# Routing and ranking for pairs of token groups, running counts on TensorE, one reciprocal buffer

## The chip, the cores and the metric

The kernel runs on 1 core of a Trainium2 chip. The metric is the device time of one execution in microseconds (us); the number quoted is the median of three runs.

## What is computed

Three stages follow each other; the first feeds the second, the second the third.

```python
# 1 attention with a decaying state: 4 batches, 8 heads, 768 tokens, 48 wide
for t in range(S):
    state = alpha[:, :, t, :, None] * state + einsum('bhd,bhe->bhde', k[:, :, t], v[:, :, t])
    y[:, :, t] = einsum('bhd,bhde->bhe', q[:, :, t], state)
# 2 gated dense block on 3072 tokens of 384
x = (((x @ w1) * (x @ w2)) @ w3) @ w_out
# 3 eight experts of 384 -> 1024 -> 384, two per token
noisy = x @ w_gate + log1p(exp(x @ w_noise)) * noise
top2 = the two largest of noisy; weights = softmax over these two
out[token] += weight * (relu(x @ ew1[e]) @ ew2[e])
```

## The kernel before

**Groups.** The 3072 tokens go through in 8 groups of 384 (three tiles of 128), two groups to a batch. For each group attention runs in three chunks: `prep_decay` and `prep_qk` (decay products as scans on VectorE), `scores`, `ktok`, `mix`, `state`, `xturn`. Then come the dense units: sixteen `wide` units of nine matmuls (L532 to L534), and six `narrow` units of twelve (L556 to L558), which give the tile `x2` with 384 outputs and 16 logits per token.

**Routing.** The last `narrow` unit of a group calls `finish`. It scales the logits (L577), splits the outputs into two halves of 16 bits (`split`, ScalarE L181 and VectorE L185) through a tile `xr` of two buffers, writes them to the table of tokens `x2s` from SP's queue (L583), and calls `route`. `route` is a chain of VectorE instructions on 128x24 tiles: logarithm, noise, the two largest, one-hot masks `oh`, weights. At its end (L645 to L648) it keeps a running count `R` per partition and expert: for each of three tiles a copy of `R` into `M[:, 1, t]` and an addition of the tile's mask to `R`.

**Ranking.** `rank(g)` is a unit of its own: two TensorE matmuls (L657, L658) turn the masks and the running counts into each token's place in its expert's list; ten VectorE instructions make addresses; six indirect DMAs on POOL's queue (L686) scatter the tokens' numbers and weights. `rank(g - 1)` stands in group g's units behind the seventh pair of `wide` units, in the last group behind the fifth; group 7 is ranked among the experts. After the scatters of group 0 `clear` zeroes the output: a memset, five DMAs of 960 KB (L518) and one of 192 KB, all on POOL's queue.

**Order.** TensorE's order is written out by hand (`manual_schedule`): attention units and dense units have costs, and a dense unit is emitted as long as the sum of dense costs stays under a bound on the sum of attention costs. `rank` counts 0.1 in that sum. The other engines' orders come from a planner that follows the program's order and its own durations. Each engine and each DMA queue runs its instructions in order. POOL also takes the low half of the score split (L183) for the later chunks; SP's queue carries the loads of the attention inputs (`pad`, L193, and `v`, L201), the writes to `x2s` and the experts' weights.

**Experts.** For each expert, weights are loaded (`es`, L854), their greatest value is found (`greatest`, VectorE L857), combined over partitions on TensorE (`over_all`, L865), and they are split in two halves (`cut_up`). These steps are dealt out one per TensorE unit by `prepare`, which puts each behind the last VectorE and ScalarE instructions issued so far. The second `greatest` of expert 0 so comes behind `route(6)`, and `over_all` stands in TensorE's order two `wide` units later.

Of the kernel before, what the change touches and what calls it, by code (L numbers as in the profile page):

```python
# [8 lines left out]
F32 = mybir.dt.float32  # L9
# [11 lines left out]
P = 128  # L21
# [64 lines left out]
def body(ctx, tc, q, k, v, alpha, mw1, mw2, mw3, mwo, wg, wn, noise, ew1, ew2, out, dbg=None):  # L86
# [25 lines left out]
    rev = const.tile([P, TG, E], F32, name="rev")  # L112
    nc.gpsimd.iota(rev, pattern=[[0, TG], [-1, E]], base=E, channel_multiplier=0,
# [27 lines left out]
    Bst = [ld.tile([P, G], F32, name=f"Bst{i}") for i in range(2)]  # L141
    Zs = [ld.tile([P, NP, 2 * D], F32, name=f"Zs{i}") for i in range(2)]
    for t in Bst + Zs:
        nc.gpsimd.memset(t, 0.0)
# [365 lines left out]
    GS, AB, X2, RT, LAST = {}, {}, {}, {}, []  # L510
# [55 lines left out]
    def finish(g, x2):  # L566
        xe = XE.pop(g)
        if g in SCL:
            nc.vector.tensor_scalar(xe, xe, SCL.pop(g)[:, 3:4], None, op0=OP.mult)
        del XT[g]  # L570
        am = X2.pop((g, "sq"))
        ami = am.bitcast(I32)
        pow2_scale(ami[:, 0], ami[:, 2], ami[:, 4])

        nc.vector.scalar_tensor_tensor(am[:, 3], xe, 1.0 / SX2, xe, op0=OP.mult, op1=OP.mult)
        nc.vector.tensor_tensor(am[:, 4], am[:, 4], am[:, 3], OP.mult)
        nc.vector.tensor_tensor(x2[:, :, DM:], x2[:, :, DM:],  # L577
                                am[:, 3, :, None].to_broadcast([P, TG, 2 * E]), OP.mult)
        for t in range(TG):
            xr = sp.tile([P, 2, DM], F16, name="xr")  # L580
            split(x2[:, t, :DM], xr[:, 0], xr[:, 1], am[:, 2, t:t + 1])
            n0 = P + (g * TG + t) * P
            nc.sync.dma_start(x2s[n0:n0 + P, :], xr.rearrange("p a d -> p (a d)"))  # L583
        route(g, x2, am)

    def log(u, ln):

        V = nc.vector
        k, m, r, t = [sp.tile([P, TG, E], F32, name=f"lg{i}", bufs=1) for i in range(4)]
# [14 lines left out]
    def route(g, x2, am):  # L604
        V = nc.vector
        sh = [P, TG, E]
        lg, zz = x2[:, :, DM:DM + E], x2[:, :, DM + E:]
        ex = sp.tile(sh, F32, name="ex", bufs=1)
        u = sp.tile(sh, F32, name="u", bufs=1)
        ln = sp.tile(sh, F32, name="ln")  # L610
        nl = sp.tile(sh, F32, name="nl")
# [3 lines left out]
        log(u, ln)  # L615
# [4 lines left out]
        V.tensor_tensor(ln, ln, nz[:, g * TG:(g + 1) * TG, :], OP.mult)  # L620
        V.tensor_tensor(nl, ln, lg, OP.add)
        oh = sp.tile([P, 2, TG, E], F32, name="oh")
        m = sp.tile([P, 2, TG], F32, name="m")
        rr = sp.tile([P, 2, TG], F32, name="rr")
        for j in range(2):
# [5 lines left out]
            if j == 0:  # L631
                V.scalar_tensor_tensor(nl, oh[:, 0], BIGNEG, nl, op0=OP.mult, op1=OP.add)
        md = sp.tile([P, 2, TG, 2], F32, name="md")
        w = sp.tile([P, 4, TG], F32, name="w")
# [4 lines left out]
        V.tensor_tensor(w[:, 3], am[:, 4], w[:, 2], OP.mult)  # L639
# [3 lines left out]
                      ids[:, None, g * TG:(g + 1) * TG].to_broadcast([P, 2, TG]))  # L643
        M = sp.tile([P, 2, TG, E], BF, name="M")
        V.tensor_tensor(M[:, 0], oh[:, 0], oh[:, 1], OP.add)  # L645
        for t in range(TG):
            V.tensor_copy(M[:, 1, t], R)
            V.tensor_tensor(R, R, M[:, 0, t], OP.add)  # L648
        RT[g] = (M, oh, rr, md)

    def rank(g):

        V = nc.vector
        sh = [P, TG, E]
# [13 lines left out]
        if g == NG - 1:  # L668

            V.tensor_tensor(rk[:, :, :NFR], rk[:, :, :NFR], skip[:, None, :].to_broadcast([P, TG, NFR]), OP.add)  # L670
        V.tensor_tensor(oh, oh, rk[:, None].to_broadcast([P, 2, TG, E]), OP.mult)
        rs = sp.tile([P, 2, TG], F32, name="rs")
        V.tensor_reduce(rs, oh, AX.X, OP.add)
        ge = sp.tile([P, 2, TG], F32, name="ge")
        V.tensor_scalar(ge, rs, float(CAP), float(OVF - CAP), op0=OP.is_ge, op1=OP.mult)
        si = sp.tile([P, 3, 2, TG], I32, name="si")
# [5 lines left out]
        ad = sp.tile([P, 2, TG], I32, name="ad")  # L682
        last = V.tensor_tensor(ad, rs, rr, OP.add)  # L683
        for j in range(2):
            for t in range(TG):
# [6 lines left out]
        if g == 0:  # L692
            clear()
# [103 lines left out]
    def mix_units():  # L797
        fu = fuse_units()
        for g in range(NG):
            for f in range(NF):  # L800
# [8 lines left out]
                if f == (RF if g == NG - 1 else RG) and g:  # L809
# [420 lines left out]
```

## Time and profile before

| | |
|---|---|
| median of 3 runs | 1000.47 us (997.56, 1000.47, 1008.58) |
| span of the profiled execution | 990.8 us; its own time outside the profiler is not listed |
| TensorE matmul | 923.5 us busy, 93% of the span, 6847 instructions |
| VectorE | 616.8 us, 62%, 1696 instructions |
| ScalarE | 460.9 us, 47% |
| POOL | 250.5 us, 25% |
| mean granted TensorE clock | 0.975 of full speed |

The span runs from the first to the last instruction of the profiled execution. The busy time of an engine over a stretch is compared with the stretch's length: what TensorE lacks there is time it waited. A row of the timeline gives start, duration, engine, line and operation, and in brackets how long the engine had been idle before it and what released it. [...]

### The profile page before, as it was taken

The page shows a single profiled execution, that of the slowest core. Times are in us where ns is not written, and L with a number is a line of the kernel's source. Part 1 is how long each engine was busy: PE and PEld are TensorE (multiplying, and loading weights), DVE is VectorE, ACT ScalarE, POOL GpSimd, SP SyncE. Part 2 cuts the span into 40 slices and gives each one's busy share as a digit, 9 for nine tenths or more (in the row PEclk, how much of TensorE's full clock was granted, in tenths as well). Part 3 has the DMA queues.
Part 4 walks back from the last instruction along what each step waited for, and adds up shares of the span by engine and source line. Part 5 has one row for each costly group of instructions (what it writes and reads, how often), then busy time and mean ns, then how long its engine had stood idle before and what let it go on. Part 6 is the DMA issues. An engine that isn't in the chain of part 4 may idle for free.

```text
span 990.8 us, 17720 instructions
## 1 busy us (share of the span) xinstructions
PE 923.5 (93%) x6847; PEld 604.1 (61%) x6847; DVE 616.8 (62%) x1696; ACT 460.9 (47%) x920; POOL 250.5 (25%) x246
## 2 busy tenths in 40 slices
PE   7879999999899998999958999999999999999996
PEld 3668767777566665766634554665556565556564
DVE  6798878676679696886756575536445453536220
ACT  3967665364555646555524534334234342433321
POOL 1211110004030402122112335234241424242313
PEclk9898999999999999999988999999999999999998
DMA  9894581516606034000202449467756485855313
GB/s 243 218 180 106 159 194 32 95 17 200 128 14 101 9 67 55 26 1 26 96 25 64 152 73 221 82 141 161 163 125 158 101 170 115 160 132 121 40 13 45
DMA packets 186069, 104.76 MB, mean 106 GB/s; under 512 B 153712, under 2 KB 171712, under 8 KB 185984
## 3 DMA queue, kind: packets, MB, share of 16 engines
q1 hardware_dynamic: 169424, 67.25, 31.0%
q0 software_dynamic: 16560, 36.37, 16.7%
q8 instruction: 54, 0.88, 0.4%
q14 instruction: 31, 0.25, 0.1%
HBM read 73.06 MB, written 20.31 MB: 94 GB/s over the span
## 4 chain that ended last, share of the span: by engine, by line
PE 53%; DVE 25%; ACT 7%; DMA 6%; issue 5%; SPq 3%; POOL 0%; another core or an unknown queue 0%; POOLq 0%; DVEq 0%; ACTq 0%
PE ps L914 5%; PE ps L915 5%; PE ps L916 5%; PE ps L904 4%; PE ps L906 4%; PE ps L905 4%; DVE esc L857 4%; DMA es<-in_moe_w_dram 3%; PE ps L532 2%; PE ps L558 2%; PE ps L556 2%; PE ps L533 2%; PE ps L557 2%; PE ps L534 2%; DVE hl L908 2%
## 5 line engine op out<-in xcount | busy, mean ns | idle before, releaser
L938 POOL DMA_INDIRECT out_dram<-ysb,mt x56 | 87.3, 1560 | 240.5 <-ACT ysb L937 136.2
L908 DVE SCALAR_TENSOR_TENSOR hl<-ps,hh 128x512 f16<-128x512 f32 (+1 forms) x128 | 74.1, 586 | 102.7 <-ACT hh L907 87.0
L904 PE MATMUL ps<-xT,eh 128*128 128x320 f16 (+1 forms) x384 | 130.1, 339 | 2.8 <-DMA xT<-xg 2.2
L906 PE MATMUL ps<-xT,el 128*128 128x320 f16 (+1 forms) x384 | 130.2, 339 | 0.0
L905 PE MATMUL ps<-xT,eh 128*128 128x320 f16 (+1 forms) x384 | 130.2, 339 | 0.0
L916 PE MATMUL ps<-eh,hl 128*128 128x384 f16 x384 | 125.2, 326 | 0.0
L915 PE MATMUL ps<-el,hh 128*128 128x384 f16 x384 | 125.2, 326 | 0.0
L914 PE MATMUL ps<-eh,hh 128*128 128x384 f16 x384 | 125.2, 326 | 0.0
L907 ACT ACTIVATE hh<-ps 128x512 f16<-128x512 f32 (+1 forms) x128 | 65.6, 515 | 107.9 <-PE ps L906 100.2
L937 ACT ACTIVATE ysb<-ps,wv 128x384 f32<-128x384 f32 (+1 forms) x56 | 32.4, 579 | 142.3 <-PE ps L916 95.7
L185 DVE SCALAR_TENSOR_TENSOR el<-es,esc,eh 128x512 f16<-128x512 f32 (+1 forms) x80 | 66.9, 854 | 41.4 <-ACT eh L181 40.1
L686 POOL DMA_INDIRECT table<-md,ad x48 | 48.6, 1012 | 157.5 <-DVE ad L683 141.5
L536 ACT ACTIVATE ab<-ps 128x384 f32<-128x384 f32 (+2 forms) x136 | 61.4, 465 | 28.0 <-PE ps L534 24.1
L857 DVE TENSOR_REDUCE esc<-es 128x1 f32<-128x1536 f32 x32 | 55.8, 1746 | 23.0 <-DMA es<-in_moe_w_dram 23.0
L183 POOL TENSOR_TENSOR sm<-sf,sm 128x512 f16<-128x512 f32 x24 | 27.9, 1183 | 165.3 <-ACT sm L181 165.2
L532 PE MATMUL ps<-xT,w1h 128*128 128x384 f16 (+2 forms) x204 | 65.9, 324 | 2.0 <-ACT ab L536 1.5
L532 PE MATMUL ps<-xT,w0h 128*128 128x384 f16 (+2 forms) x204 | 66.5, 328 | 1.1 <-ACT xT L403 1.1
L886 POOL DMA_INDIRECT xg<-x2s,mt x56 | 55.4, 989 | 47.4 <-DMA mt<-table 32.6
L533 PE MATMUL ps<-xT,w0h 128*128 128x384 f16 (+2 forms) x204 | 66.6, 328 | 0.0
L534 PE MATMUL ps<-xT,w0l 128*128 128x384 f16 (+2 forms) x204 | 66.4, 327 | 0.0
L556 PE MATMUL ps<-Wh,gh 128*128 128x400 f16 x192 | 63.9, 333 | 2.3 <-ACT gh L181 1.5
L533 PE MATMUL ps<-xT,w1h 128*128 128x384 f16 (+2 forms) x204 | 65.7, 324 | 0.0
(288 smaller groups left out, 2087.6 us busy)
## 6 DMA issues: line engine op xcount, KB each, us to landing
es<-in_moe_w_dram SPq DMA_DIRECT2D x32, 768.0 KB
s<-in_moe_w_dram POOLq DMA_DIRECT2D x16, 512.0 KB
out_dram<-zero POOLq DMA_DIRECT2D x5, 960.0 KB
v<-in_v_dram SPq DMA_DIRECT2D x24, 192.0 KB
x2s<-xr SPq DMA_DIRECT2D x24, 192.0 KB
pad<-in_alpha_dram SPq DMA_DIRECT2D x21, 192.0 KB
pad<-in_q_dram SPq DMA_DIRECT2D x21, 192.0 KB
pad<-in_k_dram SPq DMA_DIRECT2D x21, 192.0 KB
```

What stands on the lines that cost most here:

```text
L532: nc.tensor.matmul(pm, wab[i][0][:, kk, fs], xT[:, kk, cs], start=kk == 0, stop=False)
L533: nc.tensor.matmul(pm, wab[i][0][:, kk, fs], xT[:, NK + kk, cs], start=False, stop=False)
L534: nc.tensor.matmul(pm, wab[i][1][:, kk, fs], xT[:, kk, cs], start=False, stop=kk == NK - 1)
L857: nc.vector.tensor_reduce(sc[:, 5 + i:6 + i], s[i], AX.XY, OP.max, apply_absolute_value=True)
L904: nc.tensor.matmul(pm, w1h[:, kk, fs], xT[:, kk, :n], start=kk == 0, stop=False)
L905: nc.tensor.matmul(pm, w1h[:, kk, fs], xT[:, NK + kk, :n], start=False, stop=False)
L906: nc.tensor.matmul(pm, w1l[:, kk, fs], xT[:, kk, :n], start=False, stop=kk == NK - 1)
L908: nc.vector.scalar_tensor_tensor(hl[:, f], pm, 0.0, hh[:, f], op0=OP.max, op1=OP.subtract)
L914: nc.tensor.matmul(py[:n], hh[:, f, ts], w2h[:, f], start=f == 0, stop=False)
L915: nc.tensor.matmul(py[:n], hh[:, f, ts], w2l[:, f], start=False, stop=False)
L916: nc.tensor.matmul(py[:n], hl[:, f, ts], w2h[:, f], start=False, stop=f == NF - 1)
L938: i = nc.gpsimd.indirect_dma_start(out=out, out_offset=bass.IndirectOffsetOnAxis(ap=mt[:n, t, 0:1].bitcast(U32), axis=0), in_=ys[:n], in_o ...
```

## The change

Groups 0 to 5 are routed and ranked as pairs (0,1), (2,3), (4,5); groups 6 and 7 stay alone. `finish` of each group writes scaled logits and scales into tiles `lgs` and `wsc` shared by the pair; `route` is called by the second of them and works on tiles twice as wide (128x48). `rank` of a pair stands where the rank of its second group stood, in group 2, 4 or 6, and scatters twelve times; the units of `rank` in groups 1, 3 and 5 are gone. `clear` follows the scatters of the pair (0,1), so it moves from group 1 to group 2. In `route` the three copies of `R` and three additions become one copy, one reduction over the tiles and one addition; `rank` instead adds, with `ones` as weights, each tile's mask to all later tiles by one matmul per tile. The decay's reciprocals `Bst` have one buffer where they had two; most small tiles of routing have one buffer where some had two. In `log` and `rank` tiles not shown only the width changes.

```diff
-    rev = const.tile([P, TG, E], F32, name="rev")
-    nc.gpsimd.iota(rev, pattern=[[0, TG], [-1, E]], base=E, channel_multiplier=0,
+    revs = const.tile([P, 2 * TG, E], F32, name="rev")
...
-    Bst = [ld.tile([P, G], F32, name=f"Bst{i}") for i in range(2)]
+    Bst = ld.tile([P, G], F32, name="Bst")
...
-        bs = Bst[pr % 2]
+        bs = Bst
...
+        gs = batch(g)
+        n = len(gs) * TG
+        if g == gs[0]:
+            LG[gs] = (sp.tile([P, 2 * TG, 2 * E], F32, name="lgs", bufs=1)[:, :n],
+                      sp.tile([P, 2 * TG], F32, name="wsc", bufs=1)[:, :n])
+        lgs, wsc = LG[gs]
+        at = slice((g - gs[0]) * TG, (g - gs[0] + 1) * TG)
 
         nc.vector.scalar_tensor_tensor(am[:, 3], xe, 1.0 / SX2, xe, op0=OP.mult, op1=OP.mult)
-        nc.vector.tensor_tensor(am[:, 4], am[:, 4], am[:, 3], OP.mult)
-        nc.vector.tensor_tensor(x2[:, :, DM:], x2[:, :, DM:],
+        nc.vector.tensor_tensor(wsc[:, at], am[:, 4], am[:, 3], OP.mult)
+        nc.vector.tensor_tensor(lgs[:, at], x2[:, :, DM:],
                                 am[:, 3, :, None].to_broadcast([P, TG, 2 * E]), OP.mult)
...
             nc.sync.dma_start(x2s[n0:n0 + P, :], xr.rearrange("p a d -> p (a d)"))
-        route(g, x2, am)
-
-    def log(u, ln):
+        if g == gs[-1]:
+            route(gs, *LG.pop(gs))
+
+    def batch(g):
+
+        return (g,) if g >= NG - 2 else (g // 2 * 2, g // 2 * 2 + 1)
...
-    def route(g, x2, am):
+    def route(gs, lgs, wsc):
         V = nc.vector
-        sh = [P, TG, E]
-        lg, zz = x2[:, :, DM:DM + E], x2[:, :, DM + E:]
-        ex = sp.tile(sh, F32, name="ex", bufs=1)
-        u = sp.tile(sh, F32, name="u", bufs=1)
-        ln = sp.tile(sh, F32, name="ln")
-        nl = sp.tile(sh, F32, name="nl")
+        n = len(gs) * TG
+        sh = [P, n, E]
+        lg, zz = lgs[:, :, :E], lgs[:, :, E:]
+        at = slice(gs[0] * TG, gs[0] * TG + n)
...
-        M = sp.tile([P, 2, TG, E], BF, name="M")
-        V.tensor_tensor(M[:, 0], oh[:, 0], oh[:, 1], OP.add)
-        for t in range(TG):
-            V.tensor_copy(M[:, 1, t], R)
-            V.tensor_tensor(R, R, M[:, 0, t], OP.add)
-        RT[g] = (M, oh, rr, md)
+                      ids[:, None, at].to_broadcast([P, 2, n]))
+        M = sp.tile([P, 2 * TG + 1, E], BF, name="M")
+        V.tensor_copy(M[:, n], R)
+        V.tensor_tensor(M[:, :n], oh[:, 0], oh[:, 1], OP.add)
+        V.tensor_reduce(m16 := sp.tile([P, E], F32, name="mt", bufs=1), M[:, :n].rearrange("p t e -> p e t"), AX.X, OP.add)
+        V.tensor_tensor(R, R, m16, OP.add)
+        RT[gs] = (M, oh, rr, md)
...
+        gs = batch(g)
+        n = len(gs) * TG
+        sh = [P, n, E]
+        M, oh, rr, md = RT.pop(gs)
+        pk = bank(n, E)
+        nc.tensor.matmul(pk, before, M[:, :n], start=True, stop=False)
+        for t in range(n - 1):
+            nc.tensor.matmul(pk[:, t + 1:], ones, M[:, t:t + 1].to_broadcast([P, n - 1 - t, E]), start=False, stop=False)
+        nc.tensor.matmul(pk, ones, M[:, n:n + 1].to_broadcast(sh), start=False, stop=True)
+        rk = rows_of(n, 1, E, name="rk")
...
         for j in range(2):
-            for t in range(TG):
+            for t in range(n):
                 i = nc.gpsimd.indirect_dma_start(
                     out=table_rows, out_offset=bass.IndirectOffsetOnAxis(ap=ad[:, j, t:t + 1], axis=0),
                     in_=md[:, j, t, :], in_offset=None)
                 for o in scat:
                     tc.declare_no_dep(i.ins, o.ins, reason="each token's rows are its own")
                 scat.append(i)
-        if g == 0:
+        if gs[0] == 0:
             clear()
...
-                if f == (RF if g == NG - 1 else RG) and g:
+                if f == (RF if g == NG - 1 else RG) and g and batch(g) != batch(g - 1):
                     yield (0.1, (lambda g=g: LAST.append(rank(g - 1))), 0)
```

## Rows read from the trace of the kernel before

**Rows 1.** Busy time by stretch: length, PE, PEld, DVE, ACT, POOL; clock; DMA share; GB/s.

```profile
187.00:505.00 318.00, 302.50 (x2436) 209.53 (x2435) 238.69 (x838) 172.34 (x399) 69.92 (x67) 0.99 0.29 63
```

**Rows 2.** VectorE groups by line over the span: busy us, mean ns, idle before.

```profile
L238 DVE TENSOR_TENSOR_SCAN A<-A,Bst 128x384 f32<-128x384 f32 x32 | 31.0, 968 | 0.0
...
L648 DVE TENSOR_TENSOR R<-R,M 128x8 f32<-128x8 f32 x24 | 5.8, 241 | 0.2
...
L599 DVE SCALAR_TENSOR_TENSOR lg<-lg,lg 128x24 f32<-128x24 f32 x24 | 4.3, 178 | 0.4
...
L577 DVE TENSOR_TENSOR x<-x,am 128x48 f32<-128x48 f32 x8 | 1.6, 205 | 0.0
```

**Rows 3.** TensorE's timeline: its waits beside routing in groups 3 and 5.

```profile
318.62 0.49 PE L300 MATMUL ps<-Qt,Kt 48*128 48x128 f32 x4 [0.65 <-DVE Kt L247]
...
337.91 0.34 PE L556 MATMUL ps<-Wh,gh 128*128 128x400 f16 x1 [0.64 <-issue]
...
430.15 1.02 PE L369 MATMUL ps<-v,ks 128*112 128x96 f32 x8 [1.04 <-ACT ab L536]
435.87 0.38 PE L300 MATMUL ps<-Qt,Kt 48*128 48x128 f32 x2 [0.72 <-DVE Zs L393]
437.46 0.49 PE L300 MATMUL ps<-Qt,Kt 48*128 48x128 f32 x4 [0.65 <-DVE Kt L247]
```

**Rows 4.** TensorE's timeline: the wait of the last chunk's `mix`.

```profile
484.54 1.10 PE L339 MATMUL ps<-Zs,Qt 112*128 112x96 f32 x8 [1.93 <-DVE Zs L394]
```

**Rows 5.** TensorE's timeline: two waits from 250 to 260 us.

```profile
253.25 0.49 PE L402 MATMUL ps<-ident,ys 128*128 128x128 f16 x6 [1.89 <-ACT ab L536]
...
258.68 0.80 PE L300 MATMUL ps<-Qt,Kt 48*128 48x128 f32 x4 [2.00 <-DVE Kt L247]
```

**Rows 6.** ScalarE's timeline: the third split of group 1.

```profile
252.21 0.61 ACT L181 ACTIVATE xr<-x,am 128x384 f16<-128x384 f32 x1 [5.09 <-DMA x2s<-xr]
```

**Rows 7.** Stretches of 2 us as in rows 1: DMA share and clock.

```profile
250.00:252.00 2.00, 1.36 (x10) 0.78 (x8) 0.00 (x0) 0.00 (x0) 0.00 (x0) 1.00 0.84 286
252.00:254.00 2.00, 0.49 (x6) 0.37 (x6) 1.14 (x3) 1.37 (x3) 0.00 (x0) 1.00 0.04 15
...
260.00:262.00 2.00, 2.00 (x8) 0.97 (x7) 2.00 (x15) 1.62 (x5) 0.00 (x0) 0.50 1.50 163
```

**Rows 8.** SP's queue: loads and `x2s` writes of groups 1 and 2.

```profile
244.31 9.51 SPq L583 DMA_DIRECT2D x2s<-xr  x3
...
295.50 1.68 SPq L193 DMA_DIRECT2D pad<-in_alpha_dram  x3
300.61 5.74 SPq L583 DMA_DIRECT2D x2s<-xr  x3
```

**Rows 9.** POOL's timeline: clearing, scatters of rank(1), a score split.

```profile
231.74 4.77 POOL L518 DMA_DIRECT2D out_dram<-zero  x5 [0.30 <-issue]
...
281.39 1.03 POOL L686 DMA_INDIRECT table<-md,ad  x1 [2.00 <-DVE ad L683]
...
288.42 0.96 POOL L686 DMA_INDIRECT table<-md,ad  x1 [0.31 <-issue]
302.54 2.37 POOL L183 TENSOR_TENSOR sm<-sf,sm 128x512 f16<-128x512 f32 x2 [13.16 <-ACT sm L181]
```

**Rows 10.** TensorE's timeline: the `mix` that reads that score split.

```profile
322.85 0.77 PE L350 MATMUL ps<-vh,sm 128*128 128x48 f16 x24
```

**Rows 11.** TensorE's timeline: the two matmuls of rank(5) and the next.

```profile
489.01 0.18 PE L657 MATMUL ps<-M,before 128*128 128x24 bf16 x1
...
489.06 0.32 PE L532 MATMUL ps<-xT,w0h 128*128 128x384 f16 x1
```

**Rows 12.** VectorE's timeline: an addition in route(6), and the second `greatest`.

```profile
515.25 0.16 DVE L648 TENSOR_TENSOR R<-R,M 128x8 f32<-128x8 f32 x1
...
516.28 1.75 DVE L857 TENSOR_REDUCE esc<-es 128x1 f32<-128x1536 f32 x1
```

**Rows 13.** TensorE's timeline: `over_all` of expert 0.

```profile
518.28 0.16 PE L865 MATMUL ps<-em,part 128*128 128x1 bf16 x1 [10.70 <-DVE em L860]
```

More of the change, by code (lines that the diff above doesn't have):

```diff
@@ L140, in body @@
     nc.gpsimd.memset(Bend[:, P - 1::P], 1.0)
-    Bst = [ld.tile([P, G], F32, name=f"Bst{i}") for i in range(2)]
+    Bst = ld.tile([P, G], F32, name="Bst")
     Zs = [ld.tile([P, NP, 2 * D], F32, name=f"Zs{i}") for i in range(2)]
-    for t in Bst + Zs:
+    for t in [Bst] + Zs:
         nc.gpsimd.memset(t, 0.0)
@@ L509, in body @@
     scat = []
-    GS, AB, X2, RT, LAST = {}, {}, {}, {}, []
+    GS, AB, X2, RT, LG, LAST = {}, {}, {}, {}, {}, []
     def clear():
@@ L583, in finish, with rows_of, log @@
             nc.sync.dma_start(x2s[n0:n0 + P, :], xr.rearrange("p a d -> p (a d)"))
-        route(g, x2, am)
-    def log(u, ln):
+        if g == gs[-1]:
+            route(gs, *LG.pop(gs))
+    def batch(g):
+        return (g,) if g >= NG - 2 else (g // 2 * 2, g // 2 * 2 + 1)
+    def rows_of(n, *shape, dt=F32, name=None, bufs=1):
+        t = sp.tile([P, shape[0] * 2 * TG] if len(shape) == 1 else [P, shape[0] * 2 * TG * shape[1]], dt,
+                    name=name, bufs=bufs)
+        if len(shape) == 1:
+            return t[:, :shape[0] * n].rearrange("p (j t) -> p j t", t=n)
+        t = t[:, :shape[0] * n * shape[1]]
+        if shape[0] == 1:
+            return t.rearrange("p (t e) -> p t e", t=n)
+        return t.rearrange("p (j t e) -> p j t e", t=n, e=shape[1])
+    def log(u, ln, n):
         V = nc.vector
-        k, m, r, t = [sp.tile([P, TG, E], F32, name=f"lg{i}", bufs=1) for i in range(4)]
+        k, m, r, t = [rows_of(n, 1, E, name=f"lg{i}") for i in range(4)]
         V.tensor_scalar(k.bitcast(I32), u.bitcast(I32), 0x7F800000, None, op0=OP.bitwise_and)
@@ L602, in log @@
         V.scalar_tensor_tensor(ln, k, LOG2, t, op0=OP.mult, op1=OP.add)
-    def route(g, x2, am):
+    def route(gs, lgs, wsc):
         V = nc.vector
-        sh = [P, TG, E]
-        lg, zz = x2[:, :, DM:DM + E], x2[:, :, DM + E:]
-        ex = sp.tile(sh, F32, name="ex", bufs=1)
-        u = sp.tile(sh, F32, name="u", bufs=1)
-        ln = sp.tile(sh, F32, name="ln")
-        nl = sp.tile(sh, F32, name="nl")
+        n = len(gs) * TG
+        sh = [P, n, E]
+        lg, zz = lgs[:, :, :E], lgs[:, :, E:]
+        at = slice(gs[0] * TG, gs[0] * TG + n)
+        ex, u, ln, nl = [rows_of(n, 1, E, name=x) for x in ("ex", "u", "ln", "nl")]
         nc.scalar.activation(ex, zz, AF.Exp)
@@ L614, in route @@
         V.tensor_scalar(u, ex, 1.0, None, op0=OP.add)
-        log(u, ln)
+        log(u, ln, n)
         V.scalar_tensor_tensor(ex, u, 1.0, ex, op0=OP.subtract, op1=OP.subtract)
@@ L619, in route @@
         V.tensor_tensor(ln, ln, ex, OP.subtract)
-        V.tensor_tensor(ln, ln, nz[:, g * TG:(g + 1) * TG, :], OP.mult)
+        V.tensor_tensor(ln, ln, nz[:, at, :], OP.mult)
         V.tensor_tensor(nl, ln, lg, OP.add)
-        oh = sp.tile([P, 2, TG, E], F32, name="oh")
-        m = sp.tile([P, 2, TG], F32, name="m")
-        rr = sp.tile([P, 2, TG], F32, name="rr")
+        oh = rows_of(n, 2, E, name="oh")
+        m = rows_of(n, 2, name="m")
+        rr = rows_of(n, 2, name="rr")
+        rev = revs[:, :n]
         for j in range(2):
@@ L632, in route @@
                 V.scalar_tensor_tensor(nl, oh[:, 0], BIGNEG, nl, op0=OP.mult, op1=OP.add)
-        md = sp.tile([P, 2, TG, 2], F32, name="md")
-        w = sp.tile([P, 4, TG], F32, name="w")
+        md = rows_of(n, 2, 2, name="md", bufs=2)
+        w = rows_of(n, 4, name="w")
         V.tensor_tensor(w[:, 0], m[:, 1], m[:, 0], OP.subtract)
@@ L638, in route @@
         V.reciprocal(w[:, 2], w[:, 2])
-        V.tensor_tensor(w[:, 3], am[:, 4], w[:, 2], OP.mult)
+        V.tensor_tensor(w[:, 3], wsc, w[:, 2], OP.mult)
         V.tensor_copy(md[:, 0, :, 1], w[:, 3])
```

20 lines of the change are left out of this document (7 added, 13 removed).

## The prediction

> **What bounds the kernel now.** I read the busy table first: TensorE is busy 93% of the span, VectorE 62%. So a saving on VectorE counts only where TensorE waits, and I went to the stretch that the change touches, from the first `finish` to the last but one. There TensorE is busy 302.5 of 318.0 us [rows 1]: at most 15.5 us can come back, however much VectorE work goes, plus what a lowered clock costs. Next I read TensorE's timeline for each wait and asked what VectorE or ScalarE were doing just before. Three kinds stand out: short waits on attention's products and on `ab` while `route` or `rank` of one group sits between them on VectorE [rows 3]; a larger one behind the clearing of the output [rows 5]; and, outside the stretch, 10.70 us before `over_all` of expert 0 [rows 13], which comes behind `route(6)` and the second `greatest` [rows 12]. Group 6 stays alone, so this one is only shortened.
>
> **The change part by part.** All terms are against the profiled span of 990.8 us. What lies around it is not listed; the median is 9.7 us above the span, the lowest run 6.8. I carry the difference over to the median, 1000.47.
>
> *Instructions removed.* Counted from the code, `route` has 47 VectorE instructions and `rank` 10, so 8 x 57 = 456 before; after it is 44 and 10 for five batches, 5 x 54 = 270. 186 go. The 24-wide `log` instructions take 178 ns [rows 2], so about 186 x 0.178 = 33 us of VectorE. A 48-wide instruction takes 205 ns [rows 2], 27 ns more; with some 36 wide ones in a pair, 3 x 36 x 0.027 = 2.9 us come back. That is 30 us of VectorE time, nearly all beside TensorE work. On the path lie the waits where a pass now vanishes, `route(2)` and `rank(2)`, `route(4)` and `rank(4)`: 0.65 + 0.64 + 1.04 + 0.72 + 0.65 = 3.7 us [rows 3]. When they go, the next late thing there is ScalarE's copy of `ab`, whose own wait is on TensorE, so I let all 3.7 count. Bounds: nothing, if attention's products are late without routing too; all 15.5 us of [rows 1]. **-3.7.**
>
> *Wider passes* for pairs (0,1), (2,3), (4,5): 2.9 us of VectorE as above; bounds 0 (covered) and 2.9 (all in a wait). Most lies beside TensorE work; I take **+0.5**.
>
> *The order of units.* Without `rank` in groups 1, 3 and 5 the dense sum is 0.3 smaller at the end. I walked both lists by the costs in the code: some ten attention units slip behind one dense unit, and the point where attention ends stays the same, so `prepare` keeps its alignment and `over_all` its place. One slip is worth naming: the last `mix` now follows a `wide` unit that stood behind it. It waited 1.93 us for the state [rows 4]; its nine matmuls, each taken at half of the 0.32 us that one shows [rows 11] because neighbours overlap (my estimate), cover 9 x 0.16 = 1.4 of that. Bounds 0 and -1.93. **-1.4.**
>
> *Clearing moves from group 1 to group 2.* Before, its five DMAs were issued from 231.74 [rows 9]; the `x2s` writes of group 1, issued at 244.31 [rows 8], landed so late that the third split stood 5.09 us [rows 6], and the DMA share falls from 0.84 to 0.04 just then [rows 7]. [...] In group 2, twelve scatters start at 281.39 and come at a pitch of (288.42 - 281.39)/5 = 1.41 [rows 9], so the last ends near 281.39 + 11 x 1.41 + 0.96 = 297.9 and the clearing begins near 298. The `x2s` writes of group 2 go out at 300.61 [rows 8]: the same collision, 58 us later. Two things differ. The loads of `pad` ahead of them on SP's queue are out at 295.50 [rows 8], before the clearing; and `route` of group 2 is no longer on VectorE, so the second wait, on `Kt`, should be shorter. Against that, the writes meet the clearing's start and not its end. I let the stand be as long as before and take 1 us off for VectorE: **-1.0** net. Bounds: -5.5 (no collision) and, from the long stand worked out below, +10.0.
>
> *Longer rows of scatters on POOL.* Behind the twelve scatters and the clearing (to about 304) a score split waits, at 302.54 before [rows 9]. Its reader on TensorE comes at 322.85 [rows 10], so some 16 us of cover remain after its own 2.37: 0. Without that cover each 1.41 us of scatter would be paid.
>
> *Running counts.* In `route(6)` the second `greatest` starts 1.03 us after the first addition to `R` begins (515.25 to 516.28) [rows 12], a chain of three additions and two copies. After, a reduction and one addition stand there, about 0.4 us by the 178 ns of [rows 2]. TensorE waits for exactly this chain [rows 13]: **-0.6** (bounds 0 and -1.0). On TensorE, `rank` has 3 x 7 + 2 x 4 = 29 matmuls for 8 x 2 = 16, 13 more. Two cost 0.05 us on the path [rows 11], so 13 x 0.025 = **+0.3**; upper bound 13 x 0.18 = 2.3.
>
> *One reciprocal buffer.* Writer and reader are both on VectorE in order, so no wait arises as long as the pairs are not interleaved; if a reciprocal had to wait for the previous scan it would cost up to 0.97 us each [rows 2]. 0. The single-buffered small tiles are nearly all written and read by VectorE: 0.
>
> Sum: -3.7 + 0.5 - 1.4 - 1.0 - 0.6 + 0.3 = -5.9 us, so a span near 985 and a time of **994.5 us**.
>
> **The rivals.**
>
> *The long stand.* The `x2s` writes wait behind the pad loads on SP's queue, and those get through only as the clearing ends. Before, the split resumed at 252.21 [rows 6], 20.5 us after the first clearing DMA [rows 9]. From 298 that is 318.5, 17.9 us after the writes go out at 300.61, where it was 7.9 before: 10.0 us longer. Those 10.0 us fall on TensorE whole, since the first part of the stand has used up its cushion already, so the term of -1.0 becomes -5.5 + 5.5 + 10.0 = +10.0 and the sum +5.1: 1005.6 us, slower than before. It decides from the point where the pad loads are not through when the clearing starts; 2.5 us lie between their issues. For it: the landing coincides with the fall of the DMA share [rows 7]. Against: the loads had a head start here that they did not have in group 1. [...] Chance 0.22.
>
> *No collision.* If group 2's pad loads and `x2s` writes get through beside the clearing, the 5.5 us do not come back: -5.9 - 4.5 = -10.4, 990.1 us. For it: the head start; against: 960 KB five times still fill the engines for some 18 us. Chance 0.18.
>
> *Nothing to gain.* Waits of VectorE were only where the last late operand happened to be; with `route` gone the scans and the score products take its place, and the clearing's cost moves unchanged. Then -0.6 - 1.4 + 0.3 + 0.5 = -1.2: 999.3 us. For it: VectorE is not full (239 of 318 us [rows 1]). Chance 0.10.
>
> **How the numbers follow.** My forecast has 0.50. Its own range, by the bounds of the waits removed (half of them to twice), is 990 to 999. The range for 8 in 10 reaches on one side to a good part of no collision, 986, and on the other to the long stand, 1006. About 1% is what a measurement can tell from no change: faster means below 990.5, slower above 1010.5. Faster: half of no collision, a sixth or so of the forecast, and a little for VectorE time worth more than its waits show: 0.24. Slower needs the long stand and a further loss of 5 us, a planner's order on VectorE that turns out badly, say: 0.08. The rest, 0.68, is within 1%.
>
> **What would show it.** Each step has a place in the profile after. VectorE's instructions fall by about 186 and its busy time by about 30 us, while TensorE's busy time stays. The waits near 253 and 259 are gone, and the clock stays at full speed there. A stand of ScalarE on `x2s` appears in group 2: about 5 us by my forecast, about 15 by the long stand, none by the third case. The waits beside groups 3 and 5 [rows 3] are absent or below 0.3 us; if others of the same size stand in their place, the case of nothing to gain was right. The wait at the last `mix` is below 0.6 us, the one before `over_all` near 10.1. I would be wrong altogether if the gain came from the experts' half, where the change has no instruction, or if TensorE's waits in the first 505 us grew.

## The result, and the profile after

The changed kernel took **1010.84 us** (median of 4 runs, 1006.97 to 1012.73); the kernel before, in runs beside it, 999.01 us (4 runs, 990.71 to 1008.58). The ratio is **1.0117**, 95% interval 1.0075 to 1.0159: slower by about 1.2% and above my range of 986 to 1006, where I had forecast 994.5. The profiled execution is that of 1009.01 us, span 1007.2.

VectorE did what the change says. Its instructions fall from 1696 to 1510, which is the 186 I had counted, but its busy time falls by 15 us (616.8 to 601.4) and not by 30. TensorE's busy time did not stay, as I had said it would: 923.5 us before, 939.2 after, with 13 instructions more and a mean clock of 0.957 for 0.975. The time went elsewhere. Set side by side by the start of the same instructions, the two traces differ like this (the last column is an execution of the same changed kernel in another job, of which more below):

| from | to | before, us | judged run, difference | `a4_again`, difference |
|---|---|---|---|---|
| start | scores of chunk 7 | 148.78 | +2.8 | +2.7 |
| scores 7 | scores 11 | 85.24 | 0.0 | 0.0 |
| scores 11 | scores 13 (the clearing's old place) | 40.40 | **-5.9** | -5.9 |
| scores 13 | scores 14 | 23.57 | +0.9 | +0.9 |
| scores 14 | scores 15 (its new place) | 19.04 | **+9.1** | -0.3 |
| scores 15 | scores 19 | 76.60 | -3.1 | +0.1 |
| scores 19 | scores 20 | 21.40 | **+9.3** | +1.5 |
| scores 20 | scores 23 | 53.49 | -5.4 | -3.3 |
| scores 23 | first `narrow` of group 6 | 23.46 | +1.7 | +0.1 |
| that | first `narrow` of group 7 | 54.96 | **+4.9** | -0.6 |
| that | first matmul of the last `layer2` | 426.11 | +2.2 | +4.2 |

Three stretches lose 23 us. Of these the forecast had only 4.5, the clearing's stall at its new place (-1.0 net for -5.5 at the old one). Busy time by stretch of the judged run, columns as in [rows 1]:

```profile
187.00:275.00 88.00, 87.67 (x671) 63.03 (x670) 61.19 (x184) 49.86 (x114) 2.50 (x3) 1.00 0.31 59
275.00:320.00 45.00, 38.31 (x286) 26.18 (x284) 30.13 (x73) 19.04 (x44) 23.85 (x23) 0.93 0.50 150
320.00:400.00 80.00, 77.01 (x653) 53.13 (x652) 60.95 (x197) 48.39 (x112) 15.08 (x13) 1.00 0.34 56
400.00:420.00 20.00, 15.65 (x102) 9.49 (x101) 11.76 (x29) 7.91 (x19) 8.98 (x10) 0.83 0.05 15
420.00:505.00 85.00, 83.08 (x706) 57.45 (x704) 61.20 (x183) 45.32 (x99) 11.93 (x11) 0.98 0.11 40
```

In the first stretch TensorE idles 0.3 of 88 us: the clearing's old stall is gone. In the second and the fourth it idles 6.7 and 4.4 us, at a lower mean clock. The timeline of TensorE shows what answers to [rows 3, 4, 5, 13]:

```profile
257.15 0.49 PE L300 MATMUL ps<-Qt,Kt 48*128 48x128 f32 x4 [0.34 <-DVE Kt L247]
...
314.48 1.81 PE L369 MATMUL ps<-v,ks 128*112 128x96 f32 x8 [4.54 <-ACT ab L536]
...
493.56 1.10 PE L339 MATMUL ps<-Zs,Qt 112*128 112x96 f32 x8 [1.92 <-DVE Zs L394]
...
532.08 0.16 PE L891 MATMUL ps<-em,part 128*128 128x1 bf16 x1 [10.30 <-DVE em L886]
```

The waits of [rows 5] are down to 0.34 us; none of the five of [rows 3] is left; the last `mix` waits as long as in [rows 4]; `over_all` waits 0.40 us less. New is the wait of 4.54 us, and something else that no step of mine had, at 406 to 411 and again at 516 to 519:

```profile
405.82 0.18 PE L350 MATMUL ps<-vh,sm 128*128 128x48 f16 x1 [0.17 <-issue]
406.56 0.25 PE L350 MATMUL ps<-vh,sm 128*128 128x48 f16 x3 [0.56 <-issue]
408.67 0.18 PE L350 MATMUL ps<-vh,sm 128*128 128x48 f16 x1 [1.86 <-issue]
409.40 0.20 PE L350 MATMUL ps<-vh,sm 128*128 128x48 f16 x1 [0.54 <-issue]
410.81 0.40 PE L350 MATMUL ps<-vh,sm 128*128 128x48 f16 x6 [1.22 <-issue]
...
516.22 0.32 PE L533 MATMUL ps<-xT,w0h 128*128 128x384 f16 x1 [1.07 <-issue]
517.63 0.32 PE L534 MATMUL ps<-xT,w0l 128*128 128x384 f16 x1 [1.09 <-issue]
518.32 0.34 PE L532 MATMUL ps<-xT,w1h 128*128 128x384 f16 x1 [0.37 <-issue]
519.03 0.50 PE L533 MATMUL ps<-xT,w1h 128*128 128x384 f16 x1 [0.38 <-issue]
```

These are matmuls in the middle of a `mix` and of a `wide`, with nothing to wait for ("issue"): the starts lie some 0.70 us, or twice or three times that, apart, where such matmuls otherwise follow each other in 0.03 us (L350) or 0.16 us (L532 to L534). At 519.03 one takes 0.50 us instead of 0.33: the granted clock has gone to 0.50, after a stretch (515.00 to 518.65) in which TensorE was busy for 1.13 of 3.65 us, and it adds to the loss: the matmuls behind it, to 521.25, follow each other in 0.32 us instead of 0.16. On POOL's timeline both places are the end of a row of twelve scatters:

```profile
393.43 1.29 POOL L712 DMA_INDIRECT table<-md,ad  x1 [3.24 <-DVE ad L709]
...
407.89 0.96 POOL L712 DMA_INDIRECT table<-md,ad  x1 [0.30 <-issue]
...
501.88 0.97 POOL L712 DMA_INDIRECT table<-md,ad  x1 [17.98 <-DVE ad L709]
...
515.79 0.96 POOL L712 DMA_INDIRECT table<-md,ad  x1 [0.31 <-issue]
```

The pacing begins 12 to 14 us after the row's first scatter and ends some 2 us after its last.

### The profile page after: what moved, and what is told of

It reads as the page before. It is cut to its first block, busy times and chain, and to the rows that moved or that the text cites. A ratio compares the mean times of both kernels' runs of the same rounds, so it can differ in the third digit from the quotient of the medians.

```text
span 1007.2 us, 17546 instructions
## 1 busy us (share of the span) xinstructions
PE 939.2 (93%) x6860; PEld 614.3 (61%) x6860; DVE 601.4 (60%) x1510; ACT 461.5 (46%) x914; POOL 253.2 (25%) x245
## 3 DMA queue, kind: packets, MB, share of 16 engines
q0 software_dynamic: 16560, 36.37, 16.3%
## 4 chain that ended last, share of the span: by engine, by line
PE 59%; DVE 21%; ACT 7%; issue 5%; DMA 4%; SPq 2%; another core or an unknown queue 1%; POOL 0%; POOLq 0%; DVEq 0%; ACTq 0%
PE ps L941 5%; PE ps L940 5%; PE ps L942 5%; PE ps L932 4%; PE ps L930 4%; PE ps L931 4%; DVE esc L883 3%; PE ps L532 3%; PE ps L534 3%; PE ps L533 3%; PE ps L558 2%; PE ps L556 2%; PE ps L557 2%; DMA es<-in_moe_w_dram 2%; PE ps L350 2%
## 5 line engine op out<-in xcount | busy, mean ns | idle before, releaser
L912 POOL DMA_INDIRECT xg<-x2s,mt x56 | 56.3, 1006 | 49.9 <-DMA mt<-table 34.3
L533 PE MATMUL ps<-xT,w1h 128*128 128x384 f16 (+2 forms) x204 | 67.5, 332 | 0.4 <-issue 0.4
L532 PE MATMUL ps<-xT,w0h 128*128 128x384 f16 (+2 forms) x204 | 66.8, 329 | 1.1 <-ACT xT L403 1.1
L532 PE MATMUL ps<-xT,w1h 128*128 128x384 f16 (+2 forms) x204 | 67.4, 331 | 0.4 <-issue 0.4
L534 PE MATMUL ps<-xT,w0l 128*128 128x384 f16 (+2 forms) x204 | 66.6, 328 | 1.1 <-issue 1.1
L534 PE MATMUL ps<-xT,w1l 128*128 128x384 f16 (+2 forms) x204 | 67.3, 331 | 0.0
```

The source lines that it names most:

```text
L532: nc.tensor.matmul(pm, wab[i][0][:, kk, fs], xT[:, kk, cs], start=kk == 0, stop=False)
L533: nc.tensor.matmul(pm, wab[i][0][:, kk, fs], xT[:, NK + kk, cs], start=False, stop=False)
L534: nc.tensor.matmul(pm, wab[i][1][:, kk, fs], xT[:, kk, cs], start=False, stop=kk == NK - 1)
```

## Experiments

Theory S: rows of twelve scatters on POOL's queue, which the change makes out of rows of six, pace the instructions of other engines near the row's end. Theory C: the clearing costs 9 us where the change puts it. Rivals: the place in TensorE's program, not the row, makes the waits; or they were one execution's own. A job, below, is a set of kernels run one after the other on one chip, with runs of the kernel before among them; ratios are to those. Kernels shown in one paragraph shared a job.

### First job: rows and clearing

`e1_split` was to hold back the second six scatters of pairs (2,3) and (4,5):

```diff
+        scatter(0)
+        if 1 < g < NG - 2: REST.append(lambda: scatter(1))   # called in the next group's unit
+        else: scatter(1)
```

> The changed kernel, but of the pairs (2,3) and (4,5) only the first six scatters stand in rank's place; the other six go to GpSimd's queue in the next group's unit ahead of its third feature block. Theory S (twelve scatters in a row pace TensorE's instructions at 0.7 us at the end of the row and drop its clock): the waits 'issue' at 405 to 411 and 516 to 519 are gone, anchors 400 to 415 cost under 2 us instead of 9.9, anchors 504 to 561 under 2 instead of 4.9; ratio to the kernel before falls from 1.012 to 0.998 to 1.004. Rival (the stalls have another cause, such as the wider passes or where the unit stands): ratio 1.009 to 1.015, the 'issue' waits stay.

Measured: **0.9987** (0.9952 to 1.0022). It fits theory S word for word, and it is worthless for it: nothing held the second six in place. In its trace the twelve scatters of a pair stand in one row as before, and every engine has the same instructions as in the changed kernel. It is the changed kernel once more, and in this job it stood 1.3% lower (0.9987 for 1.0117), without any 'issue' wait and without the 4.54 us before L369. That became the question.

`e2_twelve` adds six scatters into a spare table to the kernel before:

```diff
+        for x in range((0, 6, 6, 6, 6, 6, 0, 0)[g]):
+            j, t = divmod(x, TG)
+            i = nc.gpsimd.indirect_dma_start(out=spare_rows, ..., in_=md[:, j, t, :], ...)
```

> The kernel before, with six scatters more (into a spare table that nothing reads) behind the six of groups 1 to 5, so twelve stand in a row there. Theory S: 'issue' waits of 0.3 to 2 us on TensorE at the ends of several of the five rows, with half clock behind them, where the kernel before has none: +8 to +25 us (ratio 1.008 to 1.025). Rival (scatters are covered, the row's length costs TensorE nothing): +0 to +3 us, no 'issue' waits at the ends.

Measured: 1.0121 (1.0077 to 1.0164), in the bounds of theory S, but not one 'issue' wait stands in its trace. Between scores 7 and the first `narrow` of group 7 it is 9.7 us longer than the kernel before, and part of that shows as waits for `Zs`: 3.63 us before the last `mix` instead of 1.93 [rows 4], 1.45 at 419. One source is plain in the trace. Behind the row of group 4 a score split stands on POOL's queue; it now starts only behind the twelfth scatter, and VectorE waits for it, which it does not in the kernel before:

```profile
460.93 0.96 POOL L697 DMA_INDIRECT table<-md,ad  x1 [0.30 <-issue]
461.92 1.17 POOL L186 TENSOR_TENSOR sm<-sf,sm 128x512 f16<-128x512 f32 x1
...
463.12 0.69 DVE L310 TENSOR_TENSOR sf<-ps,csl 128x512 f32<-128x512 f32 x1 [3.66 <-POOL sm L186]
```

So a longer row can also cost time in the plain way, through POOL's own work behind it. No trace of the changed kernel has such a wait of VectorE for POOL's split.

`e3_after_noclear` and `e3_before_noclear` leave out the five transfers that zero the output (so that sums there start from what lay in memory); `x2s`'s pad rows are still zeroed:

```diff
-            for i in range(5):
-                nc.gpsimd.dma_start(out[i * rows:(i + 1) * rows]..., zero...)
```

> The changed kernel without the five transfers that zero the output (the small one that zeroes the pad rows of x2s stays); the output then sums on what lay there. Theory C (the transfers of zeros collide in group 2 with x2s and with loads): the 9.05 us between the anchors at 298 and 317 are gone, -7 to -10 us against the changed kernel, ratio to the kernel before 1.002 to 1.005. Rival (those 9 us are the scatters' too, or given back at the next wait): 1.009 to 1.013.

> The kernel before without the five transfers that zero the output. Theory C: the stall at 253 to 262 is gone, -5 to -7 us, ratio 0.993 to 0.995, so that the clearing costs about 3 us more where the change puts it. Rival (the stall is x2s and the loads alone): ratio 0.999 to 1.001.

Measured: 0.9918 (0.9894 to 0.9943) and 0.9962 (0.9934 to 0.9991). The second is on theory C's side, 4 us where I had 5 to 7, and its interval reaches the 0.993 to 0.995 of that theory but not quite its rival's 0.999 to 1.001. The first is far below what either theory gave, since both had started from 1.012 and in this job the changed kernel stood at 0.9987: against that, the zeroing costs 0.7%.

### Second job: the changed kernel again, and a quiet place for the clearing

`a2_again` is the changed kernel. `e6_quiet` issues the clearing in group 5; `e7_split_quiet` adds `e1_split`'s edit, which again leaves the program as it is, so it repeats `e6_quiet`; `e9_before_quiet` is the kernel before with the same move:

```diff
-        if gs[0] == 0:
-            clear()
...
             for f in range(NF):
+                if (g, f) == (5, 5):
+                    yield (0.0, clear, 0)
```

> The changed kernel once more, for a second profile beside the experiments. Theory S (the row of twelve scatters paces TensorE) and theory K (the row does so only where the clearing has gone before in group 2): 'issue' waits of 3 to 6 us in all again near the ends of the rows of pairs (2,3) and (4,5), the wait of 4 to 6 us before the L369 matmul of group 2 again; ratio 1.008 to 1.016. Rival (the stalls were one execution's own): the 'issue' waits are elsewhere or missing, and the ratio is under 1.006.

> The changed kernel with the clearing (all six transfers of zeros) issued in group 5's sixth feature block, near 410 us, where no load and no write of x2s is under way; its rows of twelve scatters stay. Theory C/K (the clearing in group 2 costs 9 us by its collision, and the stalls behind it go with it, as in the kernel without zeroing): ratio 0.990 to 0.996. Theory S alone: the 9 us go, the 10 to 15 us of the rows stay: 1.001 to 1.006.

> The changed kernel with both: the rows of pairs (2,3) and (4,5) split in two and the clearing near 410 us. Theory C/K: as the quiet clearing alone, 0.990 to 0.996. Theory S: 0.988 to 0.996, and 5 us or more below the quiet clearing alone.

> The kernel before with the clearing near 410 us. Theory C: the stall of 5.9 us at 253 to 262 goes and nothing comes at 410: ratio 0.993 to 0.996, as without the zeroing at all (0.9962). Rival (the zeros collide wherever they stand): 0.998 to 1.002.

Measured: 1.0124 (1.0042 to 1.0206), 1.0010 (0.9977 to 1.0044), 1.0061 (1.0019 to 1.0102), 0.9975 (0.9934 to 1.0015). `a2_again` came as theory S said, `e6_quiet` at the lower end of what S alone gave. `e9_before_quiet` lies between theory C (0.993 to 0.996) and its rival (0.998 to 1.002) and decides nothing, and `e7_split_quiet`, the same program as `e6_quiet`, shows that 0.5% between two such numbers means little. So the waits are no accident of one execution: in `a2_again` they stand at the same matmuls as in the judged run, within some ten instructions. Taking the clearing out of group 2 removes the stall there (scores 14 to 15: +7.9 in `a2_again`, +0.6 in `e6_quiet`) and leaves the waits at group 4's `mix`, as theory S alone had said. The row of pair (4,5) shows in another way. TensorE's last matmul of group 6's `narrow` starts at 503.30 in `e6_quiet`, and ScalarE takes its result only at 509.20:

```profile
509.20 0.49 ACT L562 ACTIVATE xr<-ps 128x384 f16<-128x384 f32 x1 [8.62 <-remote]
```

The twelfth scatter ended at 507.05; "remote" means that the profile names no instruction that ended the wait. The judged run has the same at 515.53 (8.69 us). It is not TensorE alone that such a row holds up. `e9_before_quiet` has two small 'issue' waits, 0.65 and 0.39 us, where the kernel before has 0.64 [rows 3] and, at 451.66, 0.40. The one at 451.66 stands 1.2 us behind a row of six scatters (its last ended at 450.50).

### Third job: the rows held apart

Now a small copy that reads the next group's gate block stands before the second six, so that they cannot move up:

```diff
+    def rest_of():
+        gate = sp.tile([P, 1], F32, name="gate", bufs=1)
+        i = nc.gpsimd.tensor_copy(gate, AB[0][:, :1])
+        with tc.issue_after(i.ins):
+            REST.pop(0)()
...
+                if f == 2 and REST:
+                    yield (0.0, rest_of, 0)
```

`e10_split` does it for the last two pairs, `e12_split_quiet` for all three with the clearing in group 5; `e2_ladder` is `e2_twelve` with (0, 2, 3, 4, 5, 6, 0, 0) scatters; `a3_again` is the control.

> The changed kernel a third time, as the control for the other runs of this job: two executions of the same instructions have stood at 1.0124 and 0.9987 on two chips, with and without the 'issue' waits at the ends of the rows of twelve scatters. If the chip shows them here: 1.008 to 1.016; if not: 0.996 to 1.002.

> The changed kernel with the second six scatters of pairs (2,3) and (4,5) held behind a small copy on GpSimd that reads the next group's gate block, so that they stand 15 us or more behind the first six. Theory S (rows of twelve pace TensorE near their end): where the control shows the 'issue' waits at 400 to 411 and 509 to 519, here they are under 1 us in all, and the run is 8 to 14 us below the control; where the control has none, no difference over 3 us. Rival (the waits belong to the place in TensorE's instructions, not to the scatters): they stay at the same matmuls.

> All three pairs' scatters in sixes and the clearing near 410 us: the change without the two things held against it. Theory S with C: ratio 0.988 to 0.995 on either kind of chip. Rival (the gain of the merged passes is nothing, or the loss is elsewhere): 0.997 to 1.003.

> The kernel before with 2, 3, 4, 5 and 6 scatters more (to a spare table) behind the six of groups 1 to 5, so that rows of 6, 8, 9, 10, 11 and 12 stand in one execution. Theory S: on a chip that shows the waits, 'issue' waits at a row's end grow with its length, from 0.4 to 0.7 us at 6 to 3 to 6 us at 12. Rival: no relation to the length.

Measured: 0.9963 (0.9931 to 0.9994), 1.0029 (0.9991 to 1.0067), 0.9966 (0.9930 to 1.0003), and 1002.74 us for the ladder's one run. No trace of this job has an 'issue' wait, the ladder's neither, so theory S was not tested, and `e12_split_quiet` lies between the two ranges I had given. `e10_split` came out 0.7% above its control, where I had no difference, for a reason of its own: the second row of pair (4,5), issued at 521, keeps `md` in use, and `route(6)` waits for it, so that the second `over_all` waits 9.07 us instead of 3.78:

```profile
531.65 0.17 DVE L672 COPY md<-ids 128x6 int32<-128x6 int32 x1 [5.20 <-DMA table<-md,ad]
```

### Fourth job: long rows by bytes or by number

`e14_mix1` and `e15_mix2` are the kernel before with six scatters more in groups 1 to 5, of 128 rows or of only 16, swapped between the two. `e13_split3` is `e12_split_quiet` with the last second row at 504 instead of 516:

```diff
-        for x in range((0, 6, 6, 6, 6, 6, 0, 0)[g]):
+        m = (0, P, 16, P, 16, P, 0, 0)[g]          # e15: (0, 16, P, 16, P, 16, 0, 0)
+        for x in range(6 if m else 0):
...  ap=ad[:m, j, t:t + 1] ... in_=md[:m, j, t, :]
```

> The changed kernel with all three pairs' scatters in two rows of six, the last second row at 500 us rather than 521 so that route(6) doesn't wait for it, and the clearing near 410 us. Theory S (rows of twelve pace the engines' instructions on some chips): no 'issue' wait over 0.8 us and a ratio of 0.990 to 0.997 on either kind of chip. Rival (place in TensorE's instructions): on a chip where the other two kernels of this job show 'issue' waits, they stand here at the L350 matmuls of group 4's mix too, and the ratio is 1.000 to 1.008.

> The kernel before with six scatters more to a spare table behind the six of groups 1 to 5, of 128 rows for groups 1, 3 and 5 and of 16 rows for 2 and 4. Theory S, by the packets moved: on a chip with the waits, 'issue' or 'remote' waits of 2 to 6 us at the ends of the rows of groups 1, 3 and 5, under 1 us at those of 2 and 4. Theory S, by the number of instructions: 2 to 6 us at all five. Place rival: where they stand does not go with either.

> The same with 16 rows for groups 1, 3 and 5 and 128 for 2 and 4. By packets: 2 to 6 us at the ends of the rows of 2 and 4 alone. By instructions: at all five. Place rival: the waits stand at the same matmuls as in the other mix.

Measured: `e13_split3` **0.9939** (0.9903 to 0.9975); `e14_mix1` 1030.57 and `e15_mix2` 1027.30 us, one run each, where the kernel before has a median of 999.19. TensorE's timeline of `e14_mix1`, cut to the larger waits; the rows in groups 2 to 5 began at 335.73 (16 rows in the second six), 397.10 (128), 457.79 (16) and 517.87 (128):

```profile
345.85 0.33 PE L561 MATMUL ps<-Wh,gl 128*128 128x400 f16 x1 [0.95 <-issue]
...
350.83 0.33 PE L560 MATMUL ps<-Wl,gh 128*128 128x400 f16 x1 [1.44 <-issue]
...
410.75 0.24 PE L353 MATMUL ps<-vh,sm 128*128 128x48 f16 x3 [1.22 <-issue]
412.88 0.28 PE L353 MATMUL ps<-vh,sm 128*128 128x48 f16 x3 [1.89 <-issue]
...
470.00 0.37 PE L405 MATMUL ps<-ident,ys 128*128 128x128 f16 x2 [1.07 <-issue]
...
474.26 0.37 PE L303 MATMUL ps<-Qt,Kt 48*128 48x128 f32 x1 [1.14 <-issue]
...
534.31 0.48 PE L537 MATMUL ps<-xT,w0l 128*128 128x384 f16 x1 [1.61 <-issue]
```

and of `e15_mix2`, rows begun at 337.58 (128), 396.24 (16), 457.57 (128) and 515.70 (16):

```profile
347.69 0.33 PE L559 MATMUL ps<-Wh,gh 128*128 128x400 f16 x1 [0.81 <-issue]
...
413.39 0.32 PE L353 MATMUL ps<-vh,sm 128*128 128x48 f16 x4 [1.20 <-issue]
...
473.37 2.67 PE L303 MATMUL ps<-Qt,Kt 48*128 48x128 f32 x11 [1.53 <-issue]
...
530.63 0.32 PE L536 MATMUL ps<-xT,w0h 128*128 128x384 f16 x1 [1.72 <-issue]
```

Two things to see. The rows cause the waits: the kernel before has, in the judged job, two small ones, both under 0.7 us, and with longer rows it has them at the end of every row, in `narrow`, `mix`, a transposition, `scores` and `wide` alike (the first row, group 1's, shows 0.46 at most, far from the 2 to 6 us of the forecast). Not all of the 28 to 31 us by which the two stand above 999.19 are the waits': `e2_twelve`, with rows as long and no such wait, stood 12 us above the kernel before. And thin rows do it as well as full ones: in groups 2 to 5 the longest wait by a row's end is 1.14 to 1.72 us for the four thin rows and 0.81 to 1.89 us for the four full ones. So in these two traces it goes by the number of scatters, not by what they move. What it is in a scatter that holds the engines, no run shows.

With rows of six, `e13_split3` keeps three waits, of at most 0.93 us (I had said 0.8), at the end of the second row of pair (2,3):

```profile
414.56 0.18 PE L350 MATMUL ps<-vh,sm 128*128 128x48 f16 x1 [0.39 <-issue]
415.31 0.33 PE L541 MATMUL ps<-xT,w0h 128*128 128x384 f16 x1 [0.58 <-issue]
416.73 0.32 PE L543 MATMUL ps<-xT,w0l 128*128 128x384 f16 x1 [0.93 <-issue]
```

### Fifth job: is there a cost where there are no waits?

`a4_again` is the changed kernel, `e13_again` the split one.

> The changed kernel as the control of the next run. On a job whose traces hold the landing times of the scatters (as the two jobs without 'issue' waits did): 0.996 to 0.999. On one whose traces lack them (as those with the waits did): 1.008 to 1.016.

> All three pairs' scatters in rows of six and the clearing near 410 us, beside its control. Theory S, with the waits bound to the jobs that lack landing times: where the control has the waits, 10 to 20 us below it (0.991 to 0.997); where it has none, within 4 us of it, since the rows then cost TensorE nothing. Rival (the rows of twelve always cost, the waits are only where it shows): 8 us or more below the control on either kind.

Measured: 0.9946 (0.9912 to 0.9979), a little better than the 0.996 to 0.999 of the forecast, and 0.9943 (0.9910 to 0.9977), no 'issue' wait in either. The rows of twelve cost nothing here, and the split wins nothing. This was the same chip as the fourth job's, so it is not the chip that makes the difference.

What goes with it is seen in the list of DMA issues (the last column is the median time from issue to landing). `a2_again`, 200 to 560 us:

```profile
table<-md,ad POOLq DMA_INDIRECT x42
```

and `a4_again`, the same program and stretch:

```profile
table<-md,ad POOLq DMA_INDIRECT x42, 2.1
```

The first trace has too few records of landings to give a time. All nine traces without a landing time for the scatters (before, the judged run, the four of the second job, the three of the fourth) have 'issue' waits of 0.3 us or more on TensorE between 200 and 562 us, from two to twenty-three, and 'remote' waits of 1 us or more on ScalarE or VectorE; all ten with one (the other three jobs) have neither. Counted in the traces of the changed kernel alone, the two with waits hold 5538 and 5641 records of landings, the three without 6938 to 6953.

## Why the prediction was wrong

**The step that failed** is the one on *longer rows of scatters on POOL*, set at 0 with "some 16 us of cover". I asked only who waits for POOL behind the row, the score split, and that part held: nobody did. What the rows do to engines that don't wait for POOL at all, I did not price. A sign of it was there to be read behind a row of six: 0.40 us of 'issue' on TensorE at 451.66, and a larger one on ScalarE:

```profile
451.65 0.49 ACT L561 ACTIVATE xr<-ps 128x384 f16<-128x384 f32 x1 [3.42 <-remote]
```

What the rows cost is read best against `a4_again`, the same program without the waits: 9.3 - 1.5 = 7.8 us at group 4's `mix` and 4.9 + 0.6 = 5.5 at group 7, half clock included. Most of the 9.1 + 0.3 = 9.4 in group 2 is theirs too, through the clearing: see next. From scores 7 to the first `narrow` of group 7 the judged run is 19.0 us longer than `a4_again`, some of the 22.7 being given back between; the forecast was missed by 1010.84 - 994.5 = 16.3.

**The clearing** (-1.0) failed in both directions. Its old stall of 5.5 us (the two waits of [rows 5], 3.9 us, and half of the 3.3 us from 258.7 to 262.0, where the granted clock of the kernel before is 0.50) went as forecast (-5.9). The new one depends on 5 us of timing. In the judged run the row of pair (0,1) ends at 296.58. TensorE's transpositions for the next `A` stand there as in `a4_again` (begun at 292.30 and 292.19, 1.15 us long), but ScalarE copies their result 4.6 us later, `finish(2)` comes 4.8 us later, and the writes go out 6.4 us behind the first zeros (POOL, SP and ScalarE, as in [rows 6, 8, 9]):

```profile
297.98 0.68 ACT L229 ACTIVATE A<-ps 128x384 f32<-128x384 f32 x1 [7.25 <-remote]
...
297.15 4.77 POOL L518 DMA_DIRECT2D out_dram<-zero  x5 [0.30 <-POOL zero L515]
...
303.57 9.43 SPq L590 DMA_DIRECT2D x2s<-xr  x3
...
311.39 0.61 ACT L181 ACTIVATE xr<-x,am 128x384 f16<-128x384 f32 x1 [5.68 <-DMA x2s<-xr]
```

In `a4_again` they go out 1.5 us behind them, and the third split stands half as long, with no wait on TensorE:

```profile
293.37 0.70 ACT L229 ACTIVATE A<-ps 128x384 f32<-128x384 f32 x1 [2.76 <-PE ps L220]
...
296.78 4.77 POOL L518 DMA_DIRECT2D out_dram<-zero  x5 [0.30 <-POOL zero L515]
...
298.32 7.00 SPq L590 DMA_DIRECT2D x2s<-xr  x3
...
303.31 0.61 ACT L181 ACTIVATE xr<-x,am 128x384 f16<-128x384 f32 x1 [2.85 <-DMA x2s<-xr]
```

So the step came out at +3.2 net in the judged run and at -5.9 - 0.3 = -6.2 in the other, near the bound of -5.5 that I had given to the rival *no collision*. The *long stand* of 15 us, for which I had only that the landing and the fall of the DMA share came together [rows 7], appeared nowhere: the loads were through, the writes themselves were late. That the delay of `finish(2)` comes from the row is argued: on TensorE and ScalarE the two traces of one program agree within 0.2 us until 292, and the copy waits until the row has ended. `e6_quiet` shows only that without the clearing there the 9 us go.

**The other steps**, in the jobs without waits, where they can be read. *Instructions removed*: 186, exactly; the two stretches from scores 15 to 19 and 20 to 23 give +0.1 - 3.3 = -3.2 us in `a4_again`, for -3.7 forecast (against the kernel before without its zeroing, whose trace has no such waits either, the two give -2.4). One of the five waits of [rows 3] was no routing wait: the 0.64 us before L556 stands in `a4_again` as 0.72 us, released by ScalarE's `gh`. VectorE's 30 us were 15; the `log` passes cost 196 ns on average where the narrow ones cost 178 [rows 2], and the rest of the difference was not followed, since it lies beside TensorE's work. *Wider passes*: scores 19 to 20 lose 1.5 us in `a4_again`, `a3_again` and `e1_split` alike, for 0.5. But `e3_before_noclear`, which has no wider passes, loses 1.6 there too, so the 1.5 can't be put down to them. *Running counts*: -0.6 between group 6 and group 7, as forecast. *One reciprocal buffer*: no wait on it appears. *The last `mix`* (-1.4) failed everywhere. The nine matmuls did move ahead of it, but VectorE's work for the same `wide` moved with them, ahead of the update that the `mix` reads; in the judged run:

```profile
490.17 0.56 DVE L540 TENSOR_TENSOR ab<-ab,ab 128x384 f32<-128x384 f32 x1 [0.20 <-ACT ab L536]
491.32 0.56 DVE L183 TENSOR_TENSOR gl<-ab,gh 128x384 f16<-128x384 f32 x1 [0.59 <-ACT gh L181]
491.79 0.86 DVE L393 SCALAR_TENSOR_TENSOR Zs<-ps,scl,Zs 48x192 f32<-48x192 f32 x2
```

I had moved a unit's matmuls and left its VectorE instructions standing.

**The sum.** From scores 7 to the first matmul of group 7's `narrow` `a4_again` gains 2.7 + 4.9 = 7.6 us, `a3_again` 8.71 - 2.69 = 6.0, for 5.9 forecast. That this comes so near is partly luck: the clearing gave 5.2 us more than forecast, and the last `mix` with its 1.4 and the 1.5 between scores 19 and 20 gave less. Against the kernel before in the same job the changed kernel without waits stands at 0.9987, 0.9963 and 0.9946, where the forecast of 994.5 is 0.994 of 1000.47: a smaller gain in all three, though the intervals of the last two reach it. The medians, 994.45, 994.94 and 992.14 us, look closer because the kernel before was itself 1 to 2.5 us faster than 1000.47 in these jobs. The two with waits stand at 1.0117 and 1.0124. Nor was the difference of 9.7 us between span and median, which I carried over, time around the span: in the runs that list both it is 1.7 to 2.1 us, so the profiled execution of before was most likely a fast one. The +2.8 before scores 7 and the +2.2 behind group 7 are not the change's: the same program has -2.7 to +2.8 at the one place and +2.2 to +9.9 at the other.

**A better version.** `e13_split3`, with the scatters in sixes and the clearing in group 5, stands at 0.9939 in a job with the waits and at 0.9943 in one without. Of the kernels measured in jobs of both kinds it is the only one that is below the kernel before in both, by 0.6%, and it is 1.8% below the changed kernel where the waits are (two jobs compared: 1.0124 and 0.9939; the two did not stand side by side in a job with waits).

**What stays open.** Why some jobs show the waits and others do not, and what paces the instructions. The waits go with traces that lack landing records, so the recording itself may take part, or one cause may bring both; no run here leaves the recording out, and none shows which. So it is also open whether an execution that nobody records would lose anything by the rows of twelve.

## What to carry to other kernels

When two batches are merged, the queue that serves them gets rows twice as long: ask what a long row does to engines that never wait for it, and look in the trace of before for a small sign at the ends of the rows that are there ("issue" in the middle of a stream of matmuls). A unit that is moved takes its instructions on every engine along; move them all on paper before counting a wait as covered. And an edit that gains or loses 1% is first to be shown to have changed the program, and then beside the unchanged one in the same job: here the same instructions differed by up to 1.8% between jobs, which is more than the change itself did in any.

## What the runs showed of the hardware that was not expected

- Rows of twelve scatters at a pitch of 1.26 us, in the six traces of one kind that have them, held TensorE to one instruction in some 0.70 us, or kept ScalarE waiting for results whose matmuls were through (4.6 us longer than in `a4_again` at 297.98; 5.6 us in `e6_quiet`). On TensorE this began 9 to 18 us after the row's start and lasted until about 2 us behind its end, weight loads and matmuls alike (three of the L350 loads start at 408.68, 410.10 and 410.81). Rows of six left 0.4 to 0.9 us on TensorE. In the ten traces of the other kind no row did this; there a longer row was seen to cost time only where POOL's own work stood behind it (`e2_twelve`, where VectorE waited 3.66 us for that work).
- Twelve scatters of which six move 16 rows did the same as twelve of 128 (longest waits of 1.14 to 1.72 and of 0.81 to 1.89 us).
- The pause is only a part of the loss: at group 4's `mix` the waits from 405.82 to 410.81 sum to 4.4 us, and the granted clock then stands at 0.50 from 409.4 to 416.3, which at half speed is up to 3.4 us more. Together that is the 7.8 us which the stretch loses against `a4_again`.
